# Transposing queries and keys of half the batches with crossbar DMAs instead of TensorE in a fused attention and feed-forward kernel

## The chip, the cores and the metric

The kernel runs on one core of one Trainium2 chip. The metric is the device time of one execution in microseconds. The time before is 361.41 us, the median of 9 runs (360.63 to 362.06).

## The reference, cut to what matters

Sparse attention (a window of 32 positions to each side, and 8 global positions that see and are seen by all) over 8 batches of 8 heads, 576 positions and 64 channels, followed by two matrix products with a sine-squared activation between them.

```python
scores = scale * np.matmul(q, k.transpose(0, 1, 3, 2))      # q, k, v: 8 x 8 x 576 x 64
mask = (np.abs(pos[:, None] - pos[None, :]) <= 32) | is_global[:, None] | is_global[None, :]
scores = np.where(mask, scores, -1000000000.0)
attn = np.exp(scores - np.max(scores, axis=-1, keepdims=True))
attn = attn / (np.sum(attn, axis=-1, keepdims=True) + 1e-09)
x = np.matmul(attn, v).transpose(0, 2, 1, 3).reshape(4608, 512)
h = x @ w_in                                                 # 512 x 2048
s = np.sin(alpha * h)
out = (h + s * s / (alpha + 1e-09)) @ w_out                  # 2048 x 512
```

## The kernel before, in words

The 4608 tokens are worked in 9 chunks of 512. A loop over the chunk number `p` runs from 0 to 8. For `p` from 1 to 7 a pass has two stretches:

- The **attention part** of batch `p` (`attention`), woven together with the second product of chunk `p - 1` (`mm2`, 16 slots of four matmuls). `run` calls the nine attention steps (`j` from -3 to 5) and after each one as many `mm2` slots as `counts` says.
- The **first layer** of chunk `p` (`mm1`, 16 slots of four matmuls, the sine on ScalarE, its square on the engine that `sq` names, and one VectorE instruction that writes `H2b`).

Pass 0 is written out by hand, and pass 8 has no attention part. The schedule is manual: every engine works in the order in which the program issues to it, and so does SP, which issues the stores of the output (L715) and the DMAs that complete the values (`shift_v` L143 and L144, `global_v` L152).

An attention step `j` issues, in this order: the product with the values for unit `j` (`stage_V`, L553, and the VectorE product L572 into `xT`), the sum of weights for unit `j + 1` (`stage_D`, L535, with two ScalarE instructions L541 and L543), the mask for unit `j + 2` (`stage_M`, L513 on VectorE), the extra work that `at` names for the step, and the scores of unit `j + 3` (`stage_Q`, L501, with the exponential L507). After the last unit `stage_G` puts the global rows into `xT` with eight GpSimd copies (L588); the first layer reads `xT`.

`stage_Q` needs queries and keys with the channels on the partitions: `qT[hp]` and `kTw[hp]`, one pair for each of four pairs of heads, the keys as 12 overlapping windows of 112. They come to SBUF with the positions on the partitions (tiles `QS` and `KS`, two buffers each, loaded and cast to bf16 by GpSimd's queue at L128). For each pair of heads `stage_T` has TensorE transpose 12 blocks of the keys into `Kps` and 12 of the queries into `qp` (L456, 96x64 each), VectorE copy the keys into `kTw` (L465), and ScalarE copy the queries into `qT` (L643). For batches 3 to 7 this is done at steps 2 to 5 of the attention part before (`at`).

In attention part `p` GpSimd issues the loads of batch `p + 1`: four for keys and queries (`kq_loads`), then three for the values (`v_loads`, L109 and L115), spread by `with_extra` four to a step from step -3 on. After them it makes the copies of the global keys and queries (`globals_in`, L444 and L448). In the first layer of chunk `p` the `shift_v` and `global_v` of batch `p + 1` are issued in slot 10. Of the squares of the first layer `sq_late` gives 11 to GpSimd, 3 to VectorE and 2 to ScalarE; `sq_first`, used in pass 0, gives 8, 6 and 2.

Of the kernel before, what the change touches and what calls it, by code (L numbers as in the profile page):

```python
# [17 lines left out]
def kernel(  # L18
# [11 lines left out]
    nc = tc.nc  # L30
    P = 128
    BF = DT.bfloat16
    F32 = DT.float32

    B, H, S, D = q.shape
# [3 lines left out]
    WIN = 32  # L39
# [4 lines left out]
    NHP = H // 2  # L44
    QB = 48
    KB = QB + 2 * WIN
    NW = S // QB
# [3 lines left out]
    TW = 96  # L51
    NTW = S // TW
# [7 lines left out]
    qkp = ctx.enter_context(tc.tile_pool(name="qkp", bufs=2))  # L60
# [16 lines left out]
    kTw = [const.tile([P, NW, P], BF, name=f"kTw{i}") for i in range(NHP)]  # L77
    qT = [const.tile([P, NW, QC], BF, name=f"qT{i}") for i in range(NHP)]
# [7 lines left out]
    H2 = {i: hpool.tile([P, NT, CH], BF, name="H2b") for i in range(2)}  # L86
# [15 lines left out]
    def v_loads(b, cuts):  # L102
        W = VW[b % 2]

        def even(h0, nh):
            Wf = W[:, 0, h0 : h0 + nh].rearrange("p h u d -> p (h u) d")
            n = nh * NU
            if b or h0:
                nc.gpsimd.dma_start(out=Wf[0:KB], in_=heads_ap(v, b, h0, -WIN, KB, 0, n))  # L109
            else:  # L110
                nc.gpsimd.dma_start(out=Wf[WIN:KB], in_=heads_ap(v, b, 0, 0, KB - WIN, 0, n))
                nc.gpsimd.dma_start(out=Wf[0:WIN, 1:n], in_=heads_ap(v, b, 0, -WIN, WIN, 1, n - 1))

        def tail():
            nc.gpsimd.dma_start(  # L115
                out=W[64 : KB - WIN, 1, :, NU - 1, :],
                in_=v[b, :, S - KB + WIN + 64 : S, :].rearrange("h p d -> p h d"),
            )

        return [partial(even, h0, nh) for h0, nh in cuts] + [tail]  # L120

    def kq_loads(b, cuts):
        QS = qkp.tile([TW, H, NTW, D], BF, name="QS")
        KS = qkp.tile([TW, H, NTW, D], BF, name="KS")
        qk[b] = (QS, KS)

        def rows(src, dst, h0, nh):
            nc.gpsimd.dma_start(  # L128
                out=dst[:, h0 : h0 + nh].rearrange("p h t d -> p (h t) d"),
                in_=heads_ap(src, b, h0, 0, TW, 0, nh * NTW),  # L130
            )

        return [partial(rows, s_, d_, h0, nh) for h0, nh in cuts for s_, d_ in ((k, KS), (q, QS))]
# [4 lines left out]
    def load_slots(b):  # L138
        return kq_loads(b, QUADS) + v_loads(b, QUADS)
# [333 lines left out]
    def T_Q(b, hp, qpool, qtag, copy):  # L473
        Qps = qpool.tile([P, S], BF, name=qtag)
        T_half(qk[b][0], b, hp, Qps)
        return partial(copy, out=qT[hp][:, :, 0:QB], in_=Qps[:].rearrange("p (i c) -> p i c", c=QB))

    def stage_T(b, hp, pool, tag):
        T_K(b, hp, Kps, nc.vector.tensor_copy)
        return T_Q(b, hp, pool, tag, nc.scalar.copy)  # L480
# [168 lines left out]
    def mm1(c, H2b, psB, sq):  # L649
        pend = []  # L650

        def add_out():
            n_, h_, s_ = pend.pop(0)
            nc.vector.scalar_tensor_tensor(  # L654
                out=H2b[:, n_, :], in0=s_[:], scalar=recipT[:, n_ : n_ + 1], in1=h_,
                op0=ALU.mult, op1=ALU.add,
            )

        slots = []
        for nt in range(NT):  # L660
            def slot(nt=nt):
                h2 = psB.tile([P, CH], F32, name="hb")
                for ci in range(CT):
                    nc.tensor.matmul(  # L664
                        out=h2[:],
                        lhsT=w_in[:, ci, nt * P : (nt + 1) * P],
                        rhs=xT[:, ci, c * CH : (c + 1) * CH],
                        start=(ci == 0), stop=(ci == CT - 1),
                    )
                Sb = spool.tile([P, CH], BF, name="Sb")  # L670
                nc.scalar.activation(  # L671
                    out=Sb[:], in_=h2[:], func=AF.Sin, scale=alphaT[:, nt : nt + 1]
                )
                S2 = spool.tile([P, CH], BF, name="S2")
                eng = sq(nt)
                if eng is nc.vector and len(pend) > 1:
                    add_out()
                if eng is nc.scalar:
                    nc.scalar.activation(out=S2[:], in_=Sb[:], func=AF.Square)
                else:  # L680
                    eng.tensor_tensor(out=S2[:], in0=Sb[:], in1=Sb[:], op=ALU.mult)  # L681
                pend.append((nt, h2[:], S2))
                if len(pend) > 2:
                    add_out()
                if nt == NT - 1:
                    while pend:
                        add_out()
            slots.append(slot)
        return slots
# [58 lines left out]
    def with_extra(parts, extra, start, per):  # L748
        for i in range(start, len(parts)):
            k_ = (i - start) * per  # L750
            if extra[k_ : k_ + per]:
                parts[i] = partial(chain, parts[i], *extra[k_ : k_ + per])
        return extra[(len(parts) - start) * per :] if len(parts) > start else extra
# [58 lines left out]
    for p in range(NCH):  # L812
        fill = []
        if p == 0:
            phase_0()
            first.close()
        elif p < B:
            with phase_pool("psA", 1) as psA:
                for tag, shape, dt_ in (
                    ("den", [P, NB, QC], F32), ("Sp", [P, 2, CH], F32), ("num", [P, NB, QC], F32),  # L820
                    ("o2", [P, DM], F32), ("qp", [P, S], BF),
                ):
                    psA.tile(shape, dt_, name=tag)
                fill = mm2(p - 1, H2[p - 1], ((psC, "ops"), (psA, "o2")) * 2)
                if p == 1:
                    fill[:8] = [fill[i] for i in (0, 1, 4, 5, 2, 6, 3, 7)]
                T_ = lambda b, hp: partial(stage_T, b, hp, psA, "qp")
                if p == 1:
                    at = {-2: [T_(1, 2)], -1: [T_(1, 3)], 5: [T_(2, 0)]}
                elif p + 1 < B:  # L830
                    at = {2 + hp: [T_(p + 1, hp)] for hp in range(NHP)}
                else:
                    at = {}
                parts = attention(p, psA, at)
                counts = [1, 1, 1, 1, 1, 1, 2, 2, 4]
                fill.pop(0)()
                fill.pop(0)()
                if p + 1 < B:
                    with_extra(parts, load_slots(p + 1), 0, 4)
                    if p < 3:  # L840
                        parts[4] = partial(chain, parts[4], partial(gather_kq, p + 1))
                    for hp in range(NHP):
                        i_ = hp + LEAD + 1
                        parts[i_] = partial(chain, parts[i_], partial(globals_in, p + 1, hp))
                run(parts, counts, fill)
        else:
            fill = mm2(p - 1, H2[p - 1], ((psC, "ops"),) * 4)
        if p == 0:
            setup.release()
            spool = ctx.enter_context(tc.tile_pool(name="spool", bufs=4))  # L850
            osbp = ctx.enter_context(tc.tile_pool(name="osbp", bufs=2))
        with phase_pool("psB", 6) as psB:
            if p > 1:
                H2[p] = hpool.tile([P, NT, CH], BF, name="H2b")
            m1 = mm1(p, H2[p], psB, sq_last if p == B else sq_first if p == 0 else sq_late)
            if p < 3:
                m1[5] = partial(chain, m1[5], partial(globals_t, p + 1, psC, "ops"))
            if p + 1 < B:
                vs = [partial(shift_v, p + 1), partial(global_v, p + 1)]
                ts = {}  # L860
                if p == 0:
                    m1[5] = partial(chain, m1[5], *vs)
                    m1[6] = partial(chain, m1[6], w_loads[3])
                    ts = {12: (1, 0), 14: (1, 1)}
                else:
                    m1[10] = partial(chain, m1[10], *vs)
                    if p == 1:
                        ts = {2: (2, 1), 5: (2, 2), 8: (2, 3)}
                for i_, (b_, hp) in ts.items():
                    m1[i_] = partial(chain, m1[i_], partial(both, stage_T, b_, hp, psC, "ops"))  # L870
            run(m1, [1, 1, 1, 0] * (NT // 4) if p == B else [0] * NT, fill if p == B else [])
            if p == NCH - 1:
                for s in mm2(p, H2[p], ((psB, "hb"), (psC, "ops"), (psB, "hb"), (psB, "hb"), (psC, "ops")), cut=True):
                    s()
# [30 lines left out]
```

The softmax here doesn't subtract the row's maximum and nothing guards it: scores larger than these inputs give would overflow.

## Time and profile before

| what | value |
|---|---|
| median of 9 runs | 361.41 us |
| the profiled execution, its own time | 362.08 us |
| its span, first to last instruction | 360.2 us |
| mean granted TensorE clock | 0.962 |
| busy, share of the span: TensorE, VectorE, ScalarE, GpSimd | 93%, 66%, 68%, 57% |
| software DMA queue (GpSimd): packets, MB | 123120, 20.04 |
| hardware DMA queue (SP): packets, MB | 9682, 14.63 |

A row of the timeline has the start in us, the duration in us, the engine, the line, the operation with output and input, and how many instructions are merged; in brackets the idle time before it and what ended it. A row of a table by stretch has the stretch, its length, the busy time of the engines with the number of instructions, the granted TensorE clock, the mean share of the DMA engines and GB/s.

### The profile page before, as it was taken

Reading aid. Unit: us, or ns where it says so; the run is one execution under the profiler, and the core shown is the slowest. Engines: PE = TensorE matmul, PEld = TensorE weight load, DVE = VectorE, ACT = ScalarE, POOL = GpSimd, SP = SyncE. Lnnn points to the kernel's source line nnn. Section 1 sums busy time; section 2 is a strip of 40 time slices with the busy share of each in tenths; the row PEclk is TensorE's granted clock in tenths of the full one; section 3 lists DMA queues with packets and bytes.
Section 4 is the critical chain, followed back from the end, with each engine's and each line's share of the span. In section 5 each row is a group of like instructions: output and inputs, shape, how many; then the busy total and the mean of one; then the engine's idle time right before and its main releaser. Section 6 shows DMA issues by size and latency. Waiting matters only on the chain.

```text
span 360.2 us, 9353 instructions
## 1 busy us (share of the span) xinstructions
PE 333.2 (93%) x3684; PEld 172.5 (48%) x3738; DVE 238.0 (66%) x527; ACT 246.0 (68%) x376; POOL 205.9 (57%) x302
## 2 busy tenths in 40 slices
PE   5588997999989999999989999999999999999996
PEld 4464444444445445544544445444544444444444
DVE  5566794748766687758764878487848864865610
ACT  3556785857886688758874888588858885845401
POOL 9858898245891589158905792479337205765000
PEclk9557998999999999999999999999999999999999
DMA  9999999931399409940994099419932001001012
GB/s 75 169 192 183 195 173 178 173 112 44 21 167 119 111 3 148 152 114 0 138 133 125 19 86 183 109 38 72 182 101 59 29 33 60 0 2 58 30 60 87
DMA packets 133149, 35.39 MB, mean 98 GB/s; under 512 B 121794, under 2 KB 126818, under 8 KB 133106
## 3 DMA queue, kind: packets, MB, share of 16 engines
q0 software_dynamic: 123120, 20.04, 78.0%
q1 hardware_dynamic: 9682, 14.63, 13.6%
q8 instruction: 29, 0.48, 0.6%
q10 hardware_dynamic: 304, 0.14, 0.1%
q14 instruction: 14, 0.11, 0.1%
HBM read 38.95 MB, written 9.44 MB: 134 GB/s over the span
## 4 chain that ended last, share of the span: by engine, by line
PE 67%; ACT 15%; DVE 6%; DMA 5%; issue 5%; POOL 1%; ACTq 0%; DVEq 0%; POOLq 0%
PE hb L664 27%; PE o L703 11%; PE ops L703 11%; DMA w_out<-in_moe_w_out_dram 4%; ACT E L507 4%; PE Sp L501 3%; PE num L553 3%; PE den L535 3%; DVE H2b L654 2%; ACT L607 2%; ACT lnd L541 2%; PE hb L703 2%; ACT Sb L671 2%; ACT L614 2%; ACT rec L543 2%
## 5 line engine op out<-in xcount | busy, mean ns | idle before, releaser
L671 ACT ACTIVATE Sb<-hb,alphaT 128x512 bf16<-128x512 f32 x144 | 97.0, 685 | 57.6 <-PE hb L664 54.2
L664 PE MATMUL hb<-xT,w_in 128*128 128x512 bf16 x564 | 127.8, 379 | 1.2 <-DVE H2b L654 0.4
L681 POOL TENSOR_TENSOR S<-Sb 128x512 bf16<-128x512 bf16 x94 | 96.2, 1043 | 48.0 <-ACT Sb L671 44.7
L654 DVE SCALAR_TENSOR_TENSOR H2b<-S,recipT,hb 128x512 bf16<-128x512 bf16 x144 | 102.5, 741 | 30.7 <-POOL S L681 30.3
L664 PEld LDWEIGHTS <-w_in 128*128 128x128 bf16 x576 | 55.7, 98 | 66.9 <-issue 0.5
L703 PEld LDWEIGHTS <-H2b 128*128 128x128 bf16 x560 | 49.8, 98 | 57.0 <-issue 3.3
L703 PE MATMUL ops<-w_out,H2b 128*128 128x512 bf16 x283 | 72.4, 383 | 2.6 <-DMA w_out<-in_moe_w_out_dram 1.5
L703 PE MATMUL o<-w_out,H2b 128*128 128x512 bf16 x203 | 50.7, 380 | 2.9 <-issue 2.5
L588 POOL COPY xT<-xg 128x4 bf16 x64 | 13.0, 203 | 67.7 <-DVE xg L586 64.1
L507 ACT ACTIVATE E<-Sp 128x896 bf16<-128x896 f32 x48 | 43.5, 907 | 8.0 <-PE Sp L501 5.3
L572 DVE TENSOR_TENSOR xT<-num,rec 128x384 bf16<-128x384 f32 (+1 forms) x60 | 26.0, 454 | 25.7 <-PE num L553 19.3
L541 ACT ACTIVATE lnd<-den 128x384 f32<-128x384 f32 x48 | 23.7, 494 | 20.5 <-PE den L535 17.4
L513 DVE TENSOR_TENSOR E<-E,MASK 128x896 bf16<-128x896 bf16 x48 | 30.3, 632 | 7.7 <-ACT E L507 6.6
L501 PE MATMUL Sp<-qT,kTw 64*128 64x56 bf16 x768 | 20.3, 190 | 9.3 <-ACT E L507 3.0
L553 PEld LDWEIGHTS <-VW 120*64 120x64 bf16 (+1 forms) x768 | 17.0, 116 | 20.7 <-issue 12.4
L543 ACT ACTIVATE rec<-lnd 128x384 f32<-128x384 f32 x48 | 25.1, 523 | 1.5
L501 PEld LDWEIGHTS <-kTw 64*128 64x128 bf16 x768 | 15.8, 96 | 20.8 <-issue 15.3
L465 DVE COPY kTw<-Kps 128x1344 bf16<-128x1344 bf16 x29 | 24.4, 841 | 0.1
L681 DVE TENSOR_TENSOR S<-Sb 128x512 bf16<-128x512 bf16 x34 | 17.6, 517 | 8.4 <-ACT Sb L671 8.4
L553 PE MATMUL num<-E,VW 120*64 120x56 bf16 (+1 forms) x720 | 20.5, 198 | 1.6 <-issue 1.3
L128 POOL DMA_DIRECT2D KS<-in_k_dram x18 | 20.8, 1153 | 0.6 <-issue 0.6
L128 POOL DMA_DIRECT2D QS<-in_q_dram x18 | 20.2, 1123 | 0.0
(133 smaller groups left out, 305.5 us busy)
## 6 DMA issues: line engine op xcount, KB each, us to landing
out_dram<-osb SPq DMA_DIRECT2D x35, 256.0 KB
KS<-in_k_dram POOLq DMA_DIRECT2D x14, 288.0 KB, 7.9
QS<-in_q_dram POOLq DMA_DIRECT2D x14, 288.0 KB, 11.9
VW<-in_v_dram POOLq DMA_DIRECT2D x12, 336.0 KB, 11.0
VW<-VW SPq DMA_DIRECT2D x7, 384.0 KB
w_in<-in_moe_w_in_dram POOLq DMA_DIRECT2D x2, 1024.0 KB
w_out<-in_moe_w_out_dram POOLq DMA_DIRECT2D x2, 1024.0 KB
VW<-VW SPq DMA_DIRECT2D x7, 240.0 KB
```

The costliest lines, as they stand in the source:

```text
L128: nc.gpsimd.dma_start(out=dst[:, h0 : h0 + nh].rearrange("p h t d -> p (h t) d"), in_=heads_ap(src, b, h0, 0, TW, 0, nh * NTW),)
L501: nc.tensor.matmul(out=Sp[:, t, m * QC : (m + 1) * QC], lhsT=kTw[hp][pr, i, :], rhs=qT[hp][pr, i, :], start=True, stop=True, skip_group_ch ...
L507: nc.scalar.activation(out=E[:], in_=Sp[:, :, 0:EW], func=AF.Exp, scale=scale)
L513: nc.vector.tensor_tensor(out=E[:], in0=E[:], in1=mk[:, None, :].to_broadcast([P, 2, EW]), op=ALU.mult)
L541: nc.scalar.activation(out=lnd[:], in_=den[:, :, 0:QB], func=AF.Ln)
L543: nc.scalar.activation(out=rec[:], in_=lnd[:], func=AF.Exp, scale=-1.0)
L553: nc.tensor.matmul(out=num[pr, m, :], lhsT=W[0:nk, i % 2, 2 * hp + t, i // 2, :], rhs=E[0:nk, t, m * QC : (m + 1) * QC], start=b > 0 or m ...
L654: nc.vector.scalar_tensor_tensor(out=H2b[:, n_, :], in0=s_[:], scalar=recipT[:, n_ : n_ + 1], in1=h_, op0=ALU.mult, op1=ALU.add,)
L664: nc.tensor.matmul(out=h2[:], lhsT=w_in[:, ci, nt * P : (nt + 1) * P], rhs=xT[:, ci, c * CH : (c + 1) * CH], start=(ci == 0), stop=(ci == ...
L671: nc.scalar.activation(out=Sb[:], in_=h2[:], func=AF.Sin, scale=alphaT[:, nt : nt + 1])
L681: eng.tensor_tensor(out=S2[:], in0=Sb[:], in1=Sb[:], op=ALU.mult)
L703: nc.tensor.matmul(out=ops[:], lhsT=H2b[:, nt, ts * P : (ts + 1) * P], rhs=w_out[:, nt, :], start=(nt == 0), stop=(nt == NT - 1),)
```

## The change

For batches 4 to 7 the transposes leave TensorE. `x_loads` loads a batch's keys or queries with six DMAs (one for each block of 96 positions) instead of two. `cross` transposes one such block of 96 x 512 with one DMA from SBUF to SBUF on SP (`dma_start_transpose`) into a tile `XT` of 128 x 4 x 576; there are six for the keys and six for the queries of a batch. `stage_X` then takes the place of `stage_T` at the same steps: three VectorE copies from SBUF for the windows of `kTw` (the ten inner windows, and the first and the last), and one ScalarE copy from SBUF for `qT`.

The transposes of batch `p + 2` are issued in slots 1 to 12 of the first layer of chunk `p`, for `p` from 2 to 5. So keys and queries are loaded a pass earlier: those of batch 4 in chunk 2 (its keys in steps 1 to 3 of the attention part, its queries in slots 0 and 1 of the first layer), those of batch `p + 2` in attention part `p` from `p` = 3 on. The values of batch `p + 1` load last in each attention part, with one large DMA and the tail instead of two and the tail. From `p` = 2 on `shift_v` and `global_v` go from slot 10 of the first layer to slot 0, ahead of the transposes, and chunk 2's squares are shared out by `sq_first`.

```diff
+    def x_loads(b, kq):
+        def rows(jt):
+            if jt == 0:
+                qk.setdefault(b, {})[1 - kq] = qkp.tile([TW, NTW, H, D], BF, name=("KS", "QS")[kq])
+            src = (k, q)[kq]
+            nc.gpsimd.dma_start(
+                out=qk[b][1 - kq][:, jt],
+                in_=bass.AP(
+                    tensor=src.tensor, offset=src.offset + (b * H * S + jt * TW) * D,
+                    ap=[[D, TW], [S * D, H], [1, D]],
+                ),
+            )
+        return [partial(rows, jt) for jt in range(NTW)]
+
+    def cross(b, kq, jt):
+        if jt == 0:
+            XT[kq] = qkp.tile([P, NHP, S], BF, name=("KS", "QS")[kq])
+        src = qk[b][1 - kq]
+        nc.sync.dma_start_transpose(
+            out=XT[kq][:, :, jt * TW : (jt + 1) * TW],
+            in_=src[:, jt].rearrange("p h d -> p (h d)"),
+        )
+
+    def stage_X(b, hp):
+        kx, qx = XT[0][:, hp], XT[1][:, hp]
...
+        nc.vector.tensor_copy(out=kTw[hp][:, 1 : NW - 1, 0:KB], in_=win(1, NW - 2))
+        nc.vector.tensor_copy(out=kTw[hp][:, 0, WIN:KB], in_=kx[:, 0 : KB - WIN])
+        nc.vector.tensor_copy(out=kTw[hp][:, NW - 1, 0 : KB - WIN], in_=kx[:, S - KB + WIN : S])
+        return partial(
+            nc.scalar.copy, out=qT[hp][:, :, 0:QB], in_=qx.rearrange("p (i c) -> p i c", c=QB)
+        )
...
-                    at = {2 + hp: [T_(p + 1, hp)] for hp in range(NHP)}
+                    at = {2 + hp: [partial(stage_X, p + 1, hp) if p > 2 else T_(p + 1, hp)] for hp in range(NHP)}
...
-                    with_extra(parts, load_slots(p + 1), 0, 4)
-                    if p < 3:
-                        parts[4] = partial(chain, parts[4], partial(gather_kq, p + 1))
+                    if p == 1:
+                        with_extra(parts, load_slots(2), 0, 4)
+                        parts[4] = partial(chain, parts[4], partial(gather_kq, 2))
+                    else:
+                        vl = v_loads(p + 1, ((0, H),))
+                        if p == 2:
+                            with_extra(parts, kq_loads(3, QUADS) + vl, 0, 4)
+                            parts[4] = partial(chain, parts[4], partial(gather_kq, 3))
+                            with_extra(parts, x_loads(4, 0), 4, 2)
+                        else:
+                            xl = x_loads(p + 2, 0) + x_loads(p + 2, 1) if p + 2 < B else []
+                            with_extra(parts, xl + vl, 0, 4)
...
-            m1 = mm1(p, H2[p], psB, sq_last if p == B else sq_first if p == 0 else sq_late)
+            m1 = mm1(p, H2[p], psB, sq_last if p == B else sq_first if p in (0, 2) else sq_late)
...
-                    m1[10] = partial(chain, m1[10], *vs)
+                    i_ = 10 if p == 1 else 0
+                    m1[i_] = partial(chain, m1[i_], *vs)
+                    if p == 2:
+                        with_extra(m1, x_loads(4, 1), 0, 3)
+                    if p > 1 and p + 2 < B:
+                        for i in range(2 * NTW):
+                            m1[1 + i] = partial(chain, m1[1 + i], partial(cross, p + 2, i // NTW, i % NTW))
```

More of the change, by code (lines that the diff above doesn't have):

```diff
@@ L476, in T_Q @@
         return partial(copy, out=qT[hp][:, :, 0:QB], in_=Qps[:].rearrange("p (i c) -> p i c", c=QB))
+    XT = {}
+    def x_loads(b, kq):
[21 more added lines that the diff above has]
+        kx, qx = XT[0][:, hp], XT[1][:, hp]
+        base = kx[:, 0:1]
+        win = lambda i0, n: bass.AP(
+            tensor=base.tensor, offset=base.offset + i0 * QB - WIN,
+            ap=[list(base.ap[0]), [QB, n], [1, KB]],
+        )
[4 more added lines that the diff above has]
+            nc.scalar.copy, out=qT[hp][:, :, 0:QB], in_=qx.rearrange("p (i c) -> p i c", c=QB)
+        )
     def stage_T(b, hp, pool, tag):
```

## The prediction

> **What bounds the kernel now.** I read the page first (engines, slices, chain), then a table of three attention parts side by side, then the timeline of parts 5 and 7, last the rows of SP's and GpSimd's queues.
>
> ```profile
> PE 333.2 (93%) x3684; PEld 172.5 (48%) x3738; DVE 238.0 (66%) x527; ACT 246.0 (68%) x376; POOL 205.9 (57%) x302
> ...
> DMA  9999999931399409940994099419932001001012
> ...
> PE 67%; ACT 15%; DVE 6%; DMA 5%; issue 5%; POOL 1%; ACTq 0%; DVEq 0%; POOLq 0%
> ```
>
> TensorE is busy for 93% and holds 67% of the chain that ended last: it is the bound. The DMA row shows one burst of loads to a pass, about two and a half 9 us slices, then nothing for at least one slice. The attention parts of batches 5, 6 and 7, from the sine's last row to the first layer's first matmul (columns: stretch, length, busy PE, PEld, DVE, ACT, POOL, clock, DMA share, GB/s):
>
> ```profile
> 207.79:229.74 21.95, 20.99 (x355) 11.55 (x359) 15.71 (x39) 16.91 (x26) 12.62 (x24) 1.00 1.46 124
> 244.52:266.45 21.93, 20.96 (x355) 11.55 (x359) 15.72 (x39) 16.92 (x26) 12.64 (x24) 1.00 1.45 123
> 281.27:300.93 19.66, 18.82 (x261) 9.16 (x263) 12.50 (x35) 14.67 (x22) 2.37 (x9) 1.00 0.12 42
> ```
>
> Part 7 prepares no next batch: no transposes, no copies into `kTw` and `qT`, no loads. It is 2.28 us shorter, and TensorE has some 0.9 us idle in all three. So this trace already holds an attention part without the transposes. The same table for L456 alone has their cost in part 5:
>
> ```profile
> 207.80:229.90 22.10, 2.96 (x96) 2.72 (x96) 1.00 1.45 123
> ```
>
> Parts 3 and 6 are like part 5; part 4 takes 23.42 us, because TensorE stops for 1.34 us at 181.42 with nothing that the profile shows to wait for ("issue").
>
> **The change part by part.** *TensorE.* In each of parts 3 to 6, 96 transposes go: 2.96 us busy in part 5, 2.28 us of length by part 7. I take 2.28, the whole difference, as the most: 4 x 2.28 = 9.1 us. What is late next shows at the end of the parts:
>
> ```profile
> 224.14 0.80 DVE L465 COPY kTw<-Kps 128x1344 bf16<-128x1344 bf16 x1
> ...
> 226.60 0.19 DVE L586 TENSOR_TENSOR xg<-gs,gr 128x32 bf16<-128x32 f32 x1
> ...
> 226.85 2.05 POOL L588 COPY xT<-xg 128x4 bf16 x8 [7.70 <-DVE xg L586]
> ...
> 229.74 13.98 PE L664 MATMUL hb<-xT,w_in 128*128 128x512 bf16 x63
> ```
>
> ```profile
> 297.63 0.56 DVE L572 TENSOR_TENSOR xT<-num,rec 128x384 bf16<-128x384 f32 x1 [0.90 <-PE num L553]
> ...
> 298.57 0.19 DVE L586 TENSOR_TENSOR xg<-gs,gr 128x32 bf16<-128x32 f32 x1
> ...
> 298.83 2.05 POOL L588 COPY xT<-xg 128x4 bf16 x8 [16.81 <-DVE xg L586]
> ...
> 300.93 13.76 PE L664 MATMUL hb<-xT,w_in 128*128 128x512 bf16 x62
> ```
>
> In part 5 GpSimd's global copies end at 228.90, 0.84 before the first layer. In part 7 they end at 300.88, 0.05 before it. Without transposes, whatever delays VectorE late in the part delays the first layer.
>
> *VectorE copies.* Four L465 copies (3.35 us a part) become twelve from SBUF. No row shows such a copy. Between ends: L465 itself moves 1344 elements in 0.84 us, so 1120 at that pace take 0.73; twice as fast, with the 0.14 us of the shortest row (a memset of 96 elements, 138 ns) as a floor, 0.44. Each edge copy (80 elements) takes about 0.16 by that memset. One head pair: 0.76 to 1.05, against 0.84 now. Set into part 7's VectorE rows, 0.76 delays `xg` by 0.1 us; 1.05 makes the third head pair end at about 298.4, and `xg` comes 0.9 us late. I take 0.76[...], so 0.1 a part, and keep 0 to 1.0.
>
> *ScalarE copies* stay, 4 x 0.63; from SBUF instead of PSUM I count them the same. Part 7 lacks them: laid into its ScalarE rows (E at 291.90, ln at 293.16 and 295.36) they push the reciprocals back by at most 0.9 us, and those are needed only by VectorE rows that wait for TensorE. Nothing; if that cover were gone, 0.6 us a part.
>
> *GpSimd.* The seven issues of a part cost 4.73 + 2.57 + 0.54 = 7.8 us. L128's rows are 0.88 us for 1152 runs and 1.18 for 2304, so an `x_loads` issue (768 runs) is about 0.78: 12 x 0.78 + 2.16 (the large values load, seen once: the 17.6 us of L109's thirteen less twelve of 1.29) + 0.54 = 12.1. The queue so reaches `globals_in` (2.6 us) 4.3 us later, at some 15 us into the part; the global copies are due at 17.6 (part 7). Hidden by 2 us. In part 2, six issues (4.7 us) go behind `gather_kq`; the queue was empty from 107.8 to 114.98, so they fit. In first layer 2, the six loads (117.2 to 121.9) stand ahead of GpSimd's first square (slot 4, about 122.5): nothing. `sq_first` there makes GpSimd take squares 11 to 14 in a row, 4 x 1.04 against 0.87 a slot, and the next part's first mask waits for VectorE behind them: 0.4 us once, between 0 and 1.5.
>
> *Loads.* The bytes and runs are the same, keys and queries a pass earlier. The values come last: in part 4 their second load was issued at 176.3 and took 11.9 us to land, 6.2 us before `shift_v` at 194.43; issued 4.3 us later in a part 2.2 shorter they land about when SP asks for them. No cost, at worst 2 us of SP's slack below. The burst of part 2 is longer by a third and runs into the first layer.
>
> *The transposes on SP* are the open price. SP now works like this:
>
> ```profile
> 212.16 18.83 SPq L715 DMA_DIRECT2D out_dram<-osb  x4
> 231.16 0.55 SPq L143 DMA_DIRECT2D VW<-VW  x1
> 231.76 0.66 SPq L144 DMA_DIRECT2D VW<-VW  x1
> 232.46 1.66 SPq L152 DMA_DIRECT2D VW<-VgX  x2
> ```
>
> `shift_v` goes right after the last store although it stands in slot 10, so slot 0 changes nothing. The twelve transposes follow at 234.1, 4.4 us after the first layer's start. Behind them on SP stand the stores of the next part (the first 19.2 us after that start, but `osb` has two buffers and the third copy into it comes at 32.8), on GpSimd the next key and query loads (which need the raw tiles read), on VectorE and ScalarE `stage_X`: keys at 25.7, queries at 26.3. With 2 us for landing, one transpose may take c = (26.3 - 4.4 - 2) / 12 = 1.66 us before anything waits.
>
> No row of this trace transposes. The nearest: SP's issues of SBUF to SBUF DMAs, 0.55 to 0.83 us; and the packets of the software queue, 78.0% of 16 x 360.2 us over 123120 = 36.5 ns each for 163 B. A block of 96 x 512, if it moves as 384 runs of 256 B, costs 384 x 36.5 ns / 16 = 0.88 us. I take c = 0.9: done at 4.4 + 10.8 + 2 = 17.2, hidden.
>
> A rule speaks against this. The Trainium skill ("VectorE: DVE Perf Modes", The three transpose paths, and its rules for kernel authors) gives 390 ns for a 128x128 block on TensorE and 1309 ns by the crossbar, and says to use TensorE where PSUM will do. The row for TensorE here is cheaper still: 12 blocks in 0.42 us. A block of 96 x 512 is three times 128x128: by the rule c = 3.9 us if nothing overlaps, twelve end at 53, 27 us late, some 25 us lost a part and a time above 450. The skill's "Advanced Engine Details and Errata" (X-Bar Transpose) instead expects 350 to 400 GB/s, 0.26 us for the 98 KB. [...]So I go by the rows, and keep 0.26 to 3.9 open.
>
> **Sum.** 4 x (2.28 - 0.1) = 8.7, less 0.4 = 8.3 us off the profiled execution's 362.08 (span 360.2 and 1.9 around it), 353.8. The median lies 0.67 lower: 353.1.
>
> **The rivals.**
> *A* (forecast, 0.46): hidden transposes, 353.1; 350.9 if the full 2.28 comes, part 4's issue gap of 1.34 goes too and the squares cost nothing.
> *B*, VectorE becomes the bound (0.12): `xg` late by 1.0 a part, or `stage_X` behind the later `globals_in` (up to 2 us): 4 x (2.28 - 1.5) - 0.4 = 2.7, 358.7. For it: 0.05 us of slack in part 7. Against: the rows leave VectorE 4 us idle.
> *C*, no change (0.05): the TensorE time becomes waiting of the same length, 361.
> *D*, slower (0.37): the transposes take longer than 1.66 us each, ScalarE stops at the first query copy, and TensorE behind it. Price 12 x (c - 1.66) a part against 2.2 gained; it decides from c = 1.84. At c = 2.1: 4 x (5.3 - 2.2) + 0.4 = 13 us, 374; and late transposes hold up the loads and so the next `shift_v` by about 6 us a pass, which would make it 393. For it: the rule above, and that no row bounds c. Against: 2.1 us is more than twice either row.
>
> **The numbers.** A measurement here can tell about 0.2% (0.7 us) from no change. Faster 0.58 (A, B), same 0.05, slower 0.37. The range goes from 350.9 to 376, into D up to c = 2.1, and leaves out 0.05 below and some 0.15 above. A and B alone: 350.9 to 360.
>
> **What would show it.** Right: L456 falls by 384 matmuls, parts 3 to 6 take about 19.8 us, SP's transposes end before the next part's first store, nobody waits for them. Wrong: ScalarE copies into `qT` or VectorE copies into `kTw` that wait for a DMA; stores at L715 that wait; `xT` (L588) ending the first layer's wait. An SP transpose row over 1.7 us is D.

## The result and the profile after

The changed kernel takes 368.06 us (median of 10 runs, 365.74 to 370.49) against 361.49 us before (31 runs). The ratio is 1.017 with a 95% interval of 1.0145 to 1.0196: slower by 1.7%, where 353.1 us (faster by 2.3%) was forecast. Ratios are taken over the fast runs alone, those within 1.5% of the fastest of their kernel, and can differ a little from the ratio of the medians. The profiled execution took 367.25 us with a span of 365.5.

The page of the changed kernel, beside the lines of before:

```profile
PE 330.1 (90%) x3306; PEld 165.2 (45%) x3354; DVE 238.0 (65%) x562; ACT 246.1 (67%) x376; POOL 216.2 (59%) x326
...
PEclk9999999999999999989999999899999999999999
...
PE 56%; ACT 8%; DMA 8%; SPq 8%; POOL 7%; DVE 6%; issue 5%; POOLq 0%; ACTq 0%; DVEq 0%
```

TensorE has fewer matmuls and is busy for 90% instead of 93%. The chain that ended last now runs for 23% of the span through DMA, SP's queue and GpSimd, which together held 6% before. A step of the clock shows in two slices.

From the first matmul of one chunk's first layer to that of the next, from chunk 2 on to chunk 7, there are five intervals; each holds a first layer and the attention part behind it (parts 3 to 7). They take 36.9, 38.2, 36.7, 36.8 and 34.4 us before, and 39.9, 39.0, 40.0, 36.3 and 34.4 after. So the intervals of parts 3 and 5 lose some 3 us each, that of part 4 loses 0.8, and that of part 6 gains half a microsecond. Two of the attention parts, 3 and 6 (column order as in the prediction's table; the first stretch begins 0.8 us before the sine's last row ends, so part 3 itself lasts 24.9 us, against 21.9 before):

```profile
130.83:156.50 25.67, 20.01 (x265) 9.64 (x267) 17.21 (x49) 17.72 (x27) 16.64 (x32) 1.00 1.24 119
...
251.87:271.83 19.96, 19.07 (x262) 9.23 (x264) 14.58 (x47) 16.94 (x26) 7.33 (x19) 1.00 0.87 101
```

Part 6 (251.87) is what the prediction described: 19.96 us against 21.93 before. It loads no keys and queries. Part 3 (130.83) does, and TensorE is busy for 20.01 of the 25.67 us of its stretch. GpSimd's timeline in part 3 says what happened:

```profile
133.65 4.62 POOL L485 DMA_DIRECT2D KS<-in_k_dram  x6 [1.38 <-DMA KS<-KS]
145.44 4.85 POOL L485 DMA_DIRECT2D QS<-in_q_dram  x6 [7.17 <-DMA QS<-QS]
150.25 2.01 POOL L109 DMA_DIRECT2D VW<-in_v_dram  x1
152.23 0.56 POOL L115 DMA_DIRECT2D VW<-in_v_dram  x1
...
154.42 2.02 POOL L628 COPY xT<-xg 128x4 bf16 x8
```

The key loads are issued by 138.27. The first query load then waits 7.17 us: it writes a tile that the last query transposes (QS<-QS) are still reading. The pool holds two buffers for the name `QS`, and in the changed kernel the raw queries and the transposed ones (`XT`) share them, so the next batch's raw queries have to go where the last ones lie. In that queue, behind the loads, stand the copies of the global keys and queries and the eight copies into `xT`. VectorE had `xg` ready at 151.15; GpSimd comes to it at 154.42. TensorE's rows at that place, SP's rows before it, and two waits of the whole kernel:

```profile
149.82 3.63 PE L743 MATMUL o<-w_out,H2b 128*128 128x512 bf16 x16
156.50 3.73 PE L704 MATMUL hb<-xT,w_in 128*128 128x512 bf16 x9 [3.06 <-POOL xT L628]
```

```profile
121.74 10.19 SPq L499 DMA_TRANSPOSE KS<-KS  x6
132.04 7.74 SPq L499 DMA_TRANSPOSE QS<-QS  x6
139.87 14.66 SPq L755 DMA_DIRECT2D out_dram<-osb  x4
160.39 0.56 SPq L143 DMA_DIRECT2D VW<-VW  x1
```

```profile
PE hb L704 <- POOL xT L628: 8.7, 3, 3.1
...
ACT qT L683 <- DMA QS<-QS: 3.9, 2, 2.1
```

The first layer waits 8.7 us in three places for GpSimd. ScalarE waits for the transposed queries twice, 3.9 us in all, and TensorE stops behind it in parts 3 and 5, for 1.82 and 2.19 us:

```profile
147.30 0.38 PE L575 MATMUL den<-E,ones 120*64 120x448 bf16 x2 [1.82 <-DVE E L553]
...
226.33 0.38 PE L575 MATMUL den<-E,ones 120*64 120x448 bf16 x2 [2.19 <-DVE E L553]
```

After two of the three stops of the first layer the clock is low. These are the stretches from the first matmul of chunks 3, 5 and 4 on (clock in the third column from the right), and chunk 4's row with its stop:

```profile
156.50:160.50 4.00, 4.00 (x11) 1.51 (x11) 0.46 (x1) 1.28 (x2) 1.04 (x1) 0.57 1.54 152
...
235.53:239.50 3.97, 3.97 (x12) 1.46 (x12) 0.23 (x1) 1.11 (x2) 1.04 (x1) 0.60 1.39 144
195.52:199.50 3.98, 3.98 (x19) 1.84 (x19) 0.83 (x2) 2.39 (x4) 2.15 (x3) 1.00 1.44 146
...
195.52 4.69 PE L704 MATMUL hb<-xT,w_in 128*128 128x512 bf16 x21 [2.61 <-POOL xT L628]
```

At the low clock TensorE does 11 or 12 matmuls in 4 us instead of 19. The first layers of chunks 3 and 5 last 15.4 and 15.3 us, that of chunk 4 13.97. The longer first layer of chunk 5 lies in the interval of part 6, which is why that interval gains so little.

### The profile page after: what moved, and what is told of

Read it like the earlier page. It is cut to its first block, busy times and chain, and to the rows that moved or that the text cites. A ratio compares the mean times of both kernels' runs of the same rounds, so it can differ in the third digit from the quotient of the medians.

```text
span 365.5 us, 8776 instructions
## 1 busy us (share of the span) xinstructions
PE 330.1 (90%) x3306; PEld 165.2 (45%) x3354; DVE 238.0 (65%) x562; ACT 246.1 (67%) x376; POOL 216.2 (59%) x326
## 4 chain that ended last, share of the span: by engine, by line
PE 56%; ACT 8%; DMA 8%; SPq 8%; POOL 7%; DVE 6%; issue 5%; POOLq 0%; ACTq 0%; DVEq 0%
PE hb L704 27%; PE ops L743 10%; SPq L499 7%; PE o L743 6%; DMA QS<-QS 5%; POOL QS L485 3%; DMA VW<-in_v_dram 3%; ACT E L547 3%; PE den L575 2%; PE Sp L541 2%; PE hb L743 2%; PE num L593 2%; DVE H2b L694 2%; ACT Sb L711 1%; ACT lnd L581 1%
## 5 line engine op out<-in xcount | busy, mean ns | idle before, releaser
L704 PE MATMUL hb<-xT,w_in 128*128 128x512 bf16 x562 | 130.9, 386 | 10.1 <-POOL xT L628 8.7
L721 POOL TENSOR_TENSOR S<-Sb 128x512 bf16<-128x512 bf16 x91 | 93.3, 1043 | 46.7 <-ACT Sb L711 42.1
L704 PEld LDWEIGHTS <-w_in 128*128 128x128 bf16 x576 | 56.5, 99 | 79.0 <-issue 15.3
L612 DVE TENSOR_TENSOR xT<-num,rec 128x384 bf16<-128x384 f32 (+1 forms) x60 | 26.9, 469 | 17.4 <-PE num L593 10.2
L628 POOL COPY xT<-xg 128x4 bf16 x64 | 13.0, 203 | 36.4 <-DVE xg L626 32.9
L485 POOL DMA_DIRECT2D QS<-in_q_dram x24 | 18.8, 793 | 20.5 <-DMA QS<-QS 20.4
L721 DVE TENSOR_TENSOR S<-Sb 128x512 bf16<-128x512 bf16 x37 | 18.7, 504 | 10.2 <-ACT Sb L711 10.1
L575 PE MATMUL den<-E,ones 120*64 120x448 bf16 x96 | 18.9, 387 | 4.8 <-DVE E L553 4.6
L485 POOL DMA_DIRECT2D KS<-in_k_dram x24 | 18.7, 788 | 6.2 <-DMA VW<-in_v_dram 3.2
```

Source lines behind the costliest of these rows:

```text
L485: nc.gpsimd.dma_start(out=qk[b][1 - kq][:, jt], in_=bass.AP(tensor=src.tensor, offset=src.offset + (b * H * S + jt * TW) * D, ap=[[D, TW], ...
L612: nc.vector.tensor_tensor(out=xT[:, hp, x0 : x0 + nb * QB].rearrange("p (u c) -> p u c", u=nb), in0=num[:, m0 : m0 + nb, 0:QB], in1=rec[:, ...
L704: nc.tensor.matmul(out=h2[:], lhsT=w_in[:, ci, nt * P : (nt + 1) * P], rhs=xT[:, ci, c * CH : (c + 1) * CH], start=(ci == 0), stop=(ci == ...
```

## The experiments

The theory after this comparison, called the GpSimd theory: the query loads wait for the late transposes, GpSimd works in order, and so its global copies, and with them the first layer, come late. Rivals: the late-tile theory (rival D of the prediction: ScalarE stops for the transposed queries), and the traffic theory (transposes and loads slow each other and everything else). Each ratio is to the kernel before on the same chip, with its 95% interval.

**e1_own_place**: the transposed queries lie in unused columns of `xT`.

```diff
-            XT[kq] = qkp.tile([P, NHP, S], BF, name=("KS", "QS")[kq])
+            XT[kq] = xT[:, :, 7 * S : 8 * S] if kq else qkp.tile([P, NHP, S], BF, name="KS")
```

> Only the transposed queries move: they lie in the part of xT that belongs to batch 7, which is not yet in use, so the query loads no longer wait until the transposes have read the tile before them. GpSimd theory (its queue stands behind those loads, and the first layer waits for its global copies): the 8.7 us in which the first layer waits for L628 go, and the low clock after them, about 3 us: 356 us. Late-tile theory (the transposed queries come too late for ScalarE, TensorE stops behind it): the transposes are as late as before, at most 2 us gained: 366. Traffic theory (transposes and loads slow each other): 368 or more, as the loads now overlap the transposes more.

Measured: 357.51 us, 0.985 (0.981 to 0.988). GpSimd's wait for QS<-QS is gone from the list, and the first layer's wait for L628 is down to 0.3 us. The late queries are still there:

```profile
ACT qT L683 <- DMA xT<-QS: 2.8, 2, 1.7
```

The new place leaves both buffers of `QS` to the raw queries. This one line, which does not touch the transposes, takes some 11 us off the changed kernel. The GpSimd theory holds; late tiles alone, and traffic, do not explain the loss.

**e8_queries_last**: only GpSimd's order in parts 3 to 5, and the sharing of the squares that goes with it.

```diff
-                            xl = x_loads(p + 2, 0) + x_loads(p + 2, 1) if p + 2 < B else []
+                            xl = x_loads(p + 2, 0) if p + 2 < B else []
                             with_extra(parts, xl + vl, 0, 4)
+                            if p + 2 < B:
+                                with_extra(parts, x_loads(p + 2, 1), 8, 6)
...
-            m1 = mm1(p, H2[p], psB, sq_last if p == B else sq_first if p in (0, 2) else sq_late)
+            m1 = mm1(p, H2[p], psB, sq_last if p == B else sq_first if p in (0, 2, 3, 4, 5) else sq_late)
```

> Nothing but GpSimd's order in parts 3 to 5: the six query loads go behind the global copies (to the end of the last attention step), where the transposes have long read the tile; the first layer of those chunks shares its squares by sq_first, so that GpSimd is not late with the first ones. The transposes and their buffers are as in the changed kernel. GpSimd theory: the first layer no longer waits for L628 (8.7 us) and no low clock follows; the late queries stay, and 1 to 2 us of late squares may come: 358 to 361 us. Late-tile theory: the transposes land no earlier, so 365 to 368.

Measured: 355.40 us, 0.984 (0.978 to 0.989), better than expected. Buffers and transposes are those of the changed kernel, and the queries are still late:

```profile
ACT qT L683 <- DMA QS<-QS: 3.0, 3, 1.2
```

But the query loads are issued where the tile has long been read, so they no longer wait, and nothing stands behind them. e1 takes the wait away by a buffer, e8 by the order in the queue. The new sharing of the squares was not run alone; e1 and e10 gain without it.

**e4_plain_copies**: plain copies on SP in place of the transposes (384 columns of each block, moved without transposing; the kernel leaves the transposing out).

```diff
-        nc.sync.dma_start_transpose(
-            out=XT[kq][:, :, jt * TW : (jt + 1) * TW],
-            in_=src[:, jt].rearrange("p h d -> p (h d)"),
+        nc.sync.dma_start(
+            out=XT[kq][0:TW, :, jt * TW : (jt + 1) * TW],
+            in_=src[:, jt].rearrange("p h d -> p (h d)")[:, 0 : NHP * TW].rearrange("p (a c) -> p a c", c=TW),
```

> The twelve transposes of a batch become plain copies from SBUF to SBUF of the same 384 runs of 192 B instead of 256 B, so queries and keys of batches 4 to 7 are not transposed, and stage_X works on 96 partitions. If it is the transposing that makes an issue last 1.25 us and the landing 5 us, SP needs 0.6 us an issue, the query loads wait little, and the time is about 356. If it is the queue and the traffic of so many small runs (traffic theory), the time stays at 366 to 368.

Measured: 352.53 us, 0.972 (0.968 to 0.976). The issues on SP, of the changed kernel and then of this one (minimum, median, maximum in ns):

```profile
L499 SPq DMA_TRANSPOSE QS<-QS x24: 1180/1207/1759, 132.0 to 256.3; - x24
```

```profile
L499 SPq DMA_DIRECT2D QS<-QS x24: 589/590/1570, 129.3 to 235.2; - x24
```

With an issue of 0.59 us in place of 1.21, and nearly all else of the change kept, the ratio is 0.972, where the prediction's sum (353.1 against 361.4) is 0.977; nobody waits for these copies. So the sum over TensorE, VectorE, ScalarE and GpSimd's own work was about right, and the price of the transposes, issue and landing together, was what was wrong.

**e5_halves**: e1 with each transpose cut in two.

```diff
+        for g in range(2):
             nc.sync.dma_start_transpose(
-                out=XT[kq][:, :, jt * TW : (jt + 1) * TW],
-                in_=src[:, jt].rearrange("p h d -> p (h d)"),
+                out=XT[kq][:, 2 * g : 2 * g + 2, jt * TW : (jt + 1) * TW],
+                in_=src[:, jt, 4 * g : 4 * g + 4].rearrange("p h d -> p (h d)"),
```

> The kernel of e1 with each transpose cut in two of 96 x 256, 24 a batch. This measures what an issue of 1.21 us is made of. If it goes by the block of data, an issue takes about 0.6 us, SP needs the same 15 us, and the time stays at 357. If it is mostly fixed, an issue takes about 1.1 us, SP needs 26 us, the queries come some 11 us later than now and 9 us after ScalarE wants them: above 385.

Measured: 412.27 us, 1.146 (1.141 to 1.152).

```profile
L500 SPq DMA_TRANSPOSE xT<-QS x48: 1184/1215/2304, 136.8 to 304.5; - x48
```

```profile
ACT qT L684 <- DMA xT<-QS: 52.1, 4, 14.4
```

Half the block costs the same issue. SP needs twice as long, and now rival D's mechanism is the loss: ScalarE waits 52.1 us for the queries.

**e10_after_pairs**: the changed kernel with two query blocks in one DMA (three a batch instead of six; `XT` of the queries is laid out by block for this).

```diff
+            if jt % 2:
+                return
+            if jt == 0:
+                XT[1] = qkp.tile([P, NTW, NHP, TW], BF, name="QS")
+            nc.sync.dma_start_transpose(
+                out=XT[1][:, jt : jt + 2].rearrange("p j a c -> p (j a) c"),
+                in_=src[:, jt : jt + 2].rearrange("p j h d -> p (j h d)"),
```

> The changed kernel with nothing changed but the queries' transposes, two blocks in one DMA of 96 x 1024, three a batch. GpSimd's order and the buffers are as in the changed kernel. GpSimd theory with the issue on SP as its cause: the queries land some 3.6 us earlier, the query loads wait 3.6 instead of 7.2 us, GpSimd's global copies end at about the time when TensorE comes to the first layer, and ScalarE waits no more: 355 to 357 us. If the landing goes by the bytes: 366 to 368.

Measured: 355.11 us, 0.982 (0.978 to 0.986), with the same bytes transposed.

```profile
L502 SPq DMA_TRANSPOSE QS<-QS x12: 1212/1229/1852, 131.5 to 237.9; - x12
```

```profile
POOL QS L485 <- DMA QS<-QS: 1.6, 1, 1.6
...
PE hb L714 <- POOL xT L638: 1.3, 2, 0.7
```

Three issues fewer a batch, between 3 and 4 us of SP, turn a loss of 1.7% into a gain of 1.8%: GpSimd's wait falls from 20.4 us (three waits) to 1.6.

**e9_query_pairs**: e8 with the queries in pairs as in e10.

> The kernel of e8 with the queries transposed two blocks at a time, 96 x 1024 in one DMA, three a batch; keys as before. An issue took 1.21 us for 96 x 512 and 1.2 for 96 x 256, so it should take about 1.2 here too: SP is done 3.6 us earlier, the queries are in time for ScalarE (they were about 2 us late), and the low clock after that stop goes. 352 to 354 us. If the landing goes by the bytes instead, the queries stay late: 355 to 356.

Measured: 352.18 us, 0.974 (0.970 to 0.978). It beats the kernel before and the changed one; the intervals of parts 3 to 6 take 35.0, 34.7, 34.9 and 34.7 us.

**e2_values_behind** and **e3_both**: `shift_v` and `global_v` behind the transposes on SP; e3 is this with e1.

```diff
-                    i_ = 10 if p == 1 else 0
+                    i_ = 10 if p == 1 else 13 if p + 2 < B else 0
```

> Only the order on SP changes: shift_v and global_v of batches 3 to 6 go from slot 0 to slot 13 of the first layer, behind the transposes, which so start about 6 us earlier in parts 3 to 5 as they no longer wait for the values to land. GpSimd theory: the query loads wait about 6 us less, most of the first layer's wait goes: 357 us. Late-tile theory: the queries come in time too, 357 to 359, but the first layer would still wait for L628 if loads are slow. Traffic theory: nothing is gained, 366 to 368.

> Both edits: transposed queries in their own place and the values' DMAs behind the transposes on SP. GpSimd and late-tile theories together: neither GpSimd nor ScalarE waits, and what the prediction summed is left: 353 to 355 us. If one of them alone were the cause, this would be no better than the better of the two edits. Traffic theory: 365 or more.

Measured: 388.27 us, 1.071 (1.066 to 1.075), and 389.49 us, 1.073 (1.067 to 1.079). Both expectations failed. TensorE now waits elsewhere (e2):

```profile
PE num L593 <- DMA VW<-VgX: 28.7, 4, 7.9
```

In chunk 2 of e2 the last copies of the global values (L152) are issued from 136.94 on, beside the next part's loads from 133.46 on, and TensorE gets them only at 145.9. The transposes did start earlier, GpSimd's first wait for QS<-QS fell to 1.54 us, and the first layer no longer waits for L628; but the values had been on time only because they stood ahead of the transposes. e2 therefore does not speak against the GpSimd theory: it moved the wait to other DMAs of SP's queue. Why those copies took until 145.9 to land was not tried.

**e7_keys_only**: keys by the crossbar, queries loaded a pass later and transposed on TensorE as before.

```diff
-                            xl = x_loads(p + 2, 0) + x_loads(p + 2, 1) if p + 2 < B else []
+                            xl = q_loads(p + 1) + (x_loads(p + 2, 0) if p + 2 < B else [])
...
-        return partial(
-            nc.scalar.copy, out=qT[hp][:, :, 0:QB], in_=qx.rearrange("p (i c) -> p i c", c=QB)
-        )
+        return T_Q(b, hp, pool, tag, nc.scalar.copy)
```

> Half the dose: for batches 4 to 7 only the keys are transposed by the crossbar (six DMAs a batch, 7.8 us of SP); the queries are loaded a pass later and transposed on TensorE as before the change. GpSimd theory: the key loads wait at most 1 us, nothing stands behind them, and half of the gain comes, 4 x 1.1: 357 us. If the transposing itself disturbed the core in proportion to its amount (traffic theory), half of the loss would come: about 364.

Measured: 360.24 us, 1.002 (0.999 to 1.005): no loss, but no gain either. The intervals of parts 4 to 6 take 36.7 us; before, those of parts 5 and 6 took as long, and only part 4's issue gap is gone. TensorE waits at its query transposes in part 3 for ScalarE to empty the one PSUM tile:

```profile
143.09 0.45 PE L456 MATMUL qp<-identb,QS 96*64 96x96 bf16 x12 [0.37 <-ACT qT L692]
...
149.03 0.45 PE L456 MATMUL qp<-identb,QS 96*64 96x96 bf16 x12 [0.63 <-ACT qT L692]
```

So half of the transposes is not worth half of the 2.28 us. That these two waits (1.0 us of the 1.1 expected) are where it went is read from the trace and was not tried with a second tile.

## Why the prediction was wrong

- *The time without TensorE's transposes* was right. Part 6 takes 19.96 us, against 21.93 before, a gain of 1.97 where 2.18 was summed; e4 and e9 end within 1 us of the forecast.
- *ScalarE's copies* were right (`qT` 0.67 us). *VectorE's* were right at their best and too low in parts 3 to 5: L511 takes 446 ns at the median (0.44 was the lower end), an edge copy (L512, L513) 170 ns at best but 290 and 194 at the median, and single copies 1.5 to 1.8 us. No price of it shows: in part 3 VectorE had `xg` ready 3.3 us before GpSimd came to it, and e9's parts 3 to 5 are about as short as part 6.
- *The step that failed* is that of the transposes on SP, "done at 4.4 + 10.8 + 2 = 17.2, hidden". It went wrong twice: the sum was 11 us too small, and the time by which it had to end was too late. As the due time it asked only when ScalarE wants the queries (26.3 us after the first layer's start), and took what else waits for the transposes, "on GpSimd the next key and query loads (which need the raw tiles read)", for free. Their due time follows from the same rows: GpSimd would come to the query loads some 5.3 us into the part, 20 us after the first layer's start. With the 2 us of slack that the prediction gave GpSimd, that is 22. A sum of 17.2 would have met it; the measured one did not.
- *Three terms of that step's sum* were too small. An issue took 1.21 us, and from one to the next 1.30, not 0.9; in batch 4, where one issue took 3.0, the twelve took 18.0 us instead of 10.8 (15.6 to 16.9 in the batches behind it). The landing after the last issue took 5 us (139.8 to 144.9), not 2; the key loads of the next batch were on their way at the same time, but that they are the reason is not shown. The start came 5.2 to 6.9 us after the first layer's, not 4.4: in chunks 3 to 5 `shift_v` waits for values that now load last, behind the loads that waited. Sum for batch 4: 5.2 + 18.0 + 5.1 = 28.3 us instead of 17.2. That is 2 us past ScalarE's due time and 6 past GpSimd's.
- *GpSimd, "hidden by 2 us"*, failed with it: the queue was costed by its issues and not by what the first blocked one holds up.
- *The rule of the skill* that speaks for TensorE ("VectorE: DVE Perf Modes", The three transpose paths) was right about the sign for this kernel and not about the size: 3.9 us for a block was three times too much. The price measured on SP is nearly a fixed one for each DMA, which neither that rule nor the rate of the other page describes. With it the change can be made to pay (e9).
- *Rival D* had the right sign. Its point of decision was an issue above 1.84 us; the loss came at 1.30, through another consumer. Its own mechanism is there, 3.9 us in the changed kernel, and it decides only in e5. For an issue of 1.30 us its own sum gives no loss; that 368.06 lies inside the stated range of 350.9 to 376, which was opened for D, is luck.
- *The low clock* was in no case of the prediction. In the profile the account is: four parts 1.97 us shorter (7.9) and part 4's issue gap gone (1.3), against 8.7 us of the first layer's waits, 4.0 us of TensorE's stops behind the late queries, and 2.8 us at the low clock. That is 6.3 us lost; the five intervals grew by 6.6 in all, and so did the median. The span grew by 5.3 only, because the profiled execution of the kernel before came to chunk 2's first layer 1.3 us later, before any transpose is issued: its clock row has 5, 5 and 7 in the second to fourth slices, where the changed kernel's has 9.

## What to carry to other kernels

When work is given to a DMA, list everyone who waits for its end, those that overwrite its source too, and give each a due time of its own; for an engine that works in order, add what stands behind the waiting instruction. Price a DMA first by the issue and count the issues: here three fewer a batch, for the same bytes, turned the sign. An instruction that would have to wait belongs at the end of its queue, where nothing stands behind it (e8).

## What was not expected of the hardware

- An issue of a transposing DMA on SP lasts 1.21 to 1.24 us for blocks of 96x256, 96x512 and 96x1024 alike, against 0.59 us for a plain copy of 96x384 from SBUF to SBUF (medians of e5, the changed kernel, e10 and e4).
- Clock: after stops of 3.06 us the granted clock was 0.57 and 0.60 for 4 us, after one of 2.61 us it stayed at 1.00. In e1 it was 0.57 in the 4 us after a stop of 1.80 us (first rows below). The Trainium skill ("TensorE: Matmul & The Clock Gate", Part 1) speaks of about 3.4 us of idle time in a free-running window. No run here shows the window; a threshold on the length of a single stop does not fit these rows.
- VectorE's copy of 1120 elements from SBUF, 0.44 us at the median, took 1.48 us at 151.07 (last row below), while GpSimd was issuing the values load. No run here separates the two.

```profile
149.06 0.39 PE L575 MATMUL den<-E,ones 120*64 120x448 bf16 x2 [1.80 <-DVE E L553]
...
149.00:153.00 4.00, 3.94 (x20) 1.31 (x22) 2.50 (x13) 3.35 (x6) 1.01 (x4) 0.57 2.20 194
```

```profile
151.07 1.48 DVE L511 COPY kTw<-KS 128x1120 bf16<-128x1120 bf16 x1
```
